# Decode attention beside an MLP on one core: the last K tile and a V tile trade places, and the MLP's first product is spread over three steps

## The chip, the core and the metric

The kernel runs on one core of a Trainium2 chip. It is one launch, and the metric is the device time of that launch in microseconds, lower being better. A core has five engines that run side by side, each with its own queue in program order: TensorE (PE in the profile; its weight loads are PEld), VectorE (DVE), ScalarE (ACT), GpSimd (POOL) and SyncE (SP). Sixteen DMA engines move data between the main memory (HBM) and the core's SBUF; an engine only issues a transfer. Matmuls write to PSUM.

## What is computed

A decode step with one new token for each of 4 sequences. The normalized input goes to two branches whose results are added to it.

```python
x = A_x                                   # [4, 1, 576], bf16
xn = _layernorm(x)
return x + _A_ref(xn, K, V, wq, wo) + _B_ref(xn, w1, w2, w3, w4)

# branch A: 32 query heads, 16 K/V heads, Dh = 128, the last W = 2048 of 8192 rows of the cache
q = (x @ wq) -> [4, 32, 1, 128]
scores = einsum(q, k) * Dh ** -0.5
o = einsum(softmax(scores), v)
A = o.reshape(4, 1, 4096) @ wo

# branch B: with one token per sequence the shifted parts of the mixer are all zeros, so x1 = x
B = x1 + gelu(_layernorm(x1) @ w3) @ w4   # 576 -> 4608 -> 576
```

## The kernel before

**Tiles.** The 16 K/V heads are taken in 8 pairs (`NPR`), called t = 0 to 7. For a pair the 2048 rows of both heads and of all 4 sequences make one K tile and one V tile of 128 partitions x 16,384 bf16, 4 MB each. They share one pool `kv` of three buffers (`NKV = 3`), given out in turn; a load waits until the tile that held its buffer before has been read out.

**Loads.** All of this kernel's large loads but wq are issued from POOL's queue, in order. `order` (L166 to L171) is the sequence of tiles: K0 K1 V0 K2 V1 K3 V2 K4 V3 K5 V4 K6 V5 K7 V6 V7, and at the end W, which stands for the last quarter of wo and the six pieces of w4. `flush_loads` (L174) issues from it as long as a counter of free buffers allows; `free_one` (L189) adds one to the counter and calls it. It is called at two points of a step: after the fourth transpose of a K tile, and after the last P*V of a V tile. So the place of a load in POOL's queue is fixed when the program is built; when it starts is decided by its wait on the reader of its buffer. `load_kv` (L123) gathers 128 rows of 32 KB by an indirect DMA. w4 takes the buffer in which w3 lay.

**A step of the loop** (L582) works on three pairs at once: K of pair t, the softmax and P*V of pair a = t - 1, and the finish of pair o = t - 2.

- `k_transpose(t, q)` (L292), q = 0 to 3: DVE turns a quarter of the K tile in 32 x 32 blocks into one of two `kt` buffers. The first quarter of the next pair is done at the end of a step.
- `k_mask` and `k_scores` (L396, L402): PE writes -1e30 where a row belongs to another sequence, then adds eight matmuls of 128 x 512 for each quarter. A pair has two score tiles in PSUM.
- `sm_max`, `sm_maxT`, `sm_neg`, `sm_back`, `sm_bias`: DVE and PE find the maximum of each head and bring it back to all partitions. `sm_exp` (L443): ACT. `sm_turn` (L452): DVE transposes the exponentials into the `pt` buffers, of which even and odd pairs have one set each. `sm_den`, `sm_rec`: the denominators.
- `pv(t, u, lo, hi)` (L471): 32 matmuls for a pair, issued as four groups of eight between the groups of scores. The result `O` is one of two PSUM buffers.
- `o_scale`, `o_turn`, `o_sum`, `o_expand`, `o_spread`, `o_pick`, `o_proj` (L480 to L530): DVE scales and adds the four parts of `O` (four instructions), PE transposes, DVE sums, and for every second pair the result is spread to four heads' rows and multiplied by a quarter of wo into the accumulator `acc`.

**The MLP's first product**: `mlp_g(r)` (L536), r = 0 to 2, are 20, 20 and 10 matmuls with w3; `mlp_turn(r)` (L551) transposes the results; `mlp_act` (L566) is the gelu, five POOL instructions and one on ACT. All of it is written into step t = 3 (`G_AT`).

**After the loop** (L651 on) come the scores of pair 7, and around them the finish of pair 5, P*V of pair 6, the softmax and P*V of pair 7, the finish of both, and the second MLP product: the matmuls of w4, into `acc` and then into two other accumulators (`sum_matmuls`), in the order in which the pieces of w4 land.

Of the kernel before, what the change touches and what calls it, by code (L numbers as in the profile page):

```python
# [22 lines left out]
def kernel(  # L23
# [143 lines left out]
    for t in range(NPR):  # L167
        order.append(("V", t))
        if t + 2 < NPR:
            order.append(("K", t + 2))  # L170
    order.append(("W", 0))  # L171
    pos = {"n": 0, "free": NKV}

    def flush_loads(upto=P):  # L174
        while pos["n"] < len(order) and pos["free"] > 0 and pos["n"] < upto:
            kind, t = order[pos["n"]]
            if kind == "W":
                load_wo(Hkv // WOQ - 1)
                load_w4()
            else:  # L180
                if kind == "V" and t % 2 == 0 and t + 2 < NPR:
                    load_wo(t // 2)
                load_kv(kind, t)
            if (kind, t) == ("V", 1):
                load_w3()
            pos["n"] += 1
            pos["free"] -= 1
# [104 lines left out]
    def k_transpose(t, q):  # L292
        src = kv_tiles["K", t][:].bitcast(I32)[:, q * QC:(q + 1) * QC, :].rearrange("p c (ib i) -> p ib c i", i=QD)
        kt = ktp.tile([P, 2, QC, QD], I32, tag="kt")
        nc.vector.transpose(out=kt[:], in_=src)  # L295
        kts[t, q] = kt
# [174 lines left out]
    def pv(t, u, lo, hi):  # L471
        if u == 0 and lo == 0:
            O_ps[t] = ps_o.tile([P, NSL, Dh], F32, tag="O", name="O")
        vn = kv_tiles["V", t][:].rearrange("p (u s c) d -> p u s c d", u=NU, s=NSL)
        for c in range(lo, hi):
            rows = slice(c % 2 * 2 * QD, (c % 2 + 1) * 2 * QD)
            nc.tensor.matmul(out=O_ps[t][rows], lhsT=pts[t % 2 * NU + u][:, c, :], rhs=vn[:, u, :, c, :],  # L477
                             start=(u == 0 and c < 2), stop=False, skip_group_check=True)

    def o_scale(t):  # L480
        o = O_ps.pop(t)
        rds = st.pop(("rd", t))
        O_sb[t] = small.tile([P, Dh], F32, tag="O_sb", name="O_sb")
        nc.vector.tensor_scalar(out=O_sb[t][:], in0=o[:, 0, :], scalar1=rds[:, 0:1], scalar2=None, op0=ALU.mult)
        for s in range(1, NSL):
            nc.vector.scalar_tensor_tensor(out=O_sb[t][:], in0=o[:, s, :], scalar=rds[:, s:s + 1], in1=O_sb[t][:],  # L486
                                           op0=ALU.mult, op1=ALU.add)

    def o_turn(t):
        oT = ps_m.tile([P, P], F32, tag="m", name="oT")  # L490
        nc.tensor.transpose(out=oT[:], in_=O_sb.pop(t)[:], identity=ident_f)
        st["oT", t] = oT

    def o_sum(t):
        oT = st.pop(("oT", t))
        k = 2 * t % WOQ
        if k == 0:
            st["on"] = small.tile([P, WOH, B], BF16, tag="on", name="on")
        with nc.allow_low_precision("summed in float32"):
            nc.vector.reduce_sum(out=st["on"][:, k * rep:(k + 2) * rep, :].rearrange("p (e r) b -> p e (r b)", e=2),  # L500
                                 in_=oT[:].rearrange("p (g e s j) -> p e j g s", g=2, e=2, s=NSL), axis=AX.XY)

    def o_expand(h):
        if h % WOQ < WOQ - 1:
            return
        on = st.pop("on")
        x = small.tile([P, B, WOH, WOD], BF16, tag="ox", name="ox")
        nc.vector.tensor_tensor(out=x[:], in0=on[:].rearrange("p h b -> p b h").unsqueeze(3).to_broadcast([P, B, WOH, WOD]),  # L508
                                in1=own[:].unsqueeze(1).unsqueeze(1).to_broadcast([P, B, WOH, WOD]), op=ALU.mult)
        st["ox"] = x  # L510
# [16 lines left out]
    def o_proj(h):  # L527
        if h % WOQ < WOQ - 1:
            return
        acc_matmuls([(op[:, i, :], wo_tiles[h // WOQ][:, i, :]) for i in range(WOR)])  # L530
# [5 lines left out]
    def mlp_g(r):  # L536
        w3 = w_tiles["w3"]
        chunks = G_CHUNKS[r * NQD:(r + 1) * NQD]
        n = chunks[0][2]
        g_ps = (ps_o if r < 2 else ps_m).tile([P, P, n], F32, tag="O" if r < 2 else "m", name="g_ps")  # L540
        for j in range(KJ + 1):
            for g, (e, i0, _) in enumerate(chunks):
                base, k = (j * F + e * (F // 2), j) if j < KJ else (KJ * F, KJ + e)
                cols = w3[:, base:base + F // 2].rearrange("p (q i) -> p q i", q=P)
                nc.tensor.matmul(out=g_ps[g * QD:(g + 1) * QD], lhsT=ln2T[:, k, :], rhs=cols[:, :, i0:i0 + n],  # L545
                                 start=(j == 0), stop=False, skip_group_check=True)
        m = len(chunks) * QD
        g_sb[r] = bigp.tile([P, P, n], F32, tag="g", name="g_sb", bufs=1)
        nc.scalar.activation(out=g_sb[r][0:m], in_=g_ps[0:m], func=ACT.Copy)

    def mlp_turn(r):  # L551
        chunks = G_CHUNKS[r * NQD:(r + 1) * NQD]
        n, m = chunks[0][2], len(chunks)
        gT_all = ps_m.tile([P, n * m, QD], F32, tag="m", name="gT_ps")
        gT_ps = gT_all[:].rearrange("p (u g) x -> p u g x", u=n)
        gs = g_sb.pop(r)
        for u in range(n):
            nc.tensor.transpose(out=gT_ps[:, u].rearrange("p g x -> p (g x)"), in_=gs[0:m * QD, :, u],  # L558
                                identity=ident_f[0:m * QD, 0:m * QD])
        if r < 2:  # L560
            dst = xs[:, r * NFH:r * NFH + 16, :].rearrange("p (g u) b -> p u g b", u=n)
        else:
            dst = xs[:].rearrange("p (g c) b -> p c g b", c=NFH)[:, 16:18]
        nc.vector.tensor_copy(out=dst, in_=gT_ps[:, :, :, 0:B])
# [15 lines left out]
    G_AT = 3  # L580
    k_transpose(0, 0)
    for t in range(NPR - 1):  # L582
        a, o = t - 1, t - 2
        if a >= 0:
            sm_max(a, 1)
        if o >= 0:
            o_scale(o)
        k_transpose(t, 1)
        if t == G_AT:
            mlp_g(0)  # L590
        k_mask(t, 0)
        k_scores(t, 0, 0)
        if a >= 0:
            sm_maxT(a)
            sm_neg(a)
        k_scores(t, 0, 1)
        if a >= 0:
            sm_back(a)
            sm_bias(a)
            sm_exp(a, 0)  # L600
            sm_exp(a, 1)
        k_transpose(t, 2)
        if t == G_AT:
            mlp_g(1)
            mlp_turn(0)
        k_scores(t, 1, 0)
        if o >= 0:
            o_turn(o)
        k_scores(t, 1, 1)
        if a >= 0:  # L610
            sm_turn(a, 0)
        if o >= 0:
            o_sum(o)
            o_expand(2 * o + 1)
        k_transpose(t, 3)
        free_one()
        if a >= 0:
            sm_turn(a, 1)
        if t == G_AT:
            mlp_g(2)  # L620
            mlp_turn(1)
        k_mask(t, 1)
        k_scores(t, 2, 0)
        if a >= 0:
            sm_den(a)
            sm_rec(a)
            pv(a, 0, 0, SC // 2)
        k_scores(t, 2, 1)
        sm_max(t, 0)
        if o >= 0:  # L630
            o_spread(2 * o + 1)
        if a >= 0:
            pv(a, 0, SC // 2, SC)
        if o >= 0:
            o_pick(2 * o + 1)
        if t == G_AT:
            mlp_turn(2)
            mlp_act()
        if t + 1 < NPR:
            k_transpose(t + 1, 0)  # L640
        k_scores(t, 3, 0)
        if a >= 0:
            pv(a, 1, 0, SC // 2)
        k_scores(t, 3, 1)
        if a >= 0:
            pv(a, 1, SC // 2, SC)
            free_one()
        if o >= 0:
            o_proj(2 * o + 1)
# [1 line left out]
    hl = NPR - 1  # L651
    a, o = hl - 1, hl - 2
    sm_max(a, 1)
    o_scale(o)
    k_transpose(hl, 1)
    k_mask(hl, 0)
    k_scores(hl, 0, 0)
# [6 lines left out]
    sm_exp(a, 1)  # L664
    k_transpose(hl, 2)
    k_scores(hl, 1, 0)
    o_turn(o)
    k_scores(hl, 1, 1)
    k_transpose(hl, 3)
    free_one()  # L670
    o_sum(o)
    o_expand(2 * o + 1)
    sm_turn(a, 0)
    k_mask(hl, 1)
    k_scores(hl, 2, 0)
# [2 lines left out]
    sm_turn(a, 1)  # L678
    k_scores(hl, 3, 0)
    k_scores(hl, 3, 1)  # L680
    sm_den(a)
    pv(a, 0, 0, SC)
    sm_max(hl, 1)
    sm_rec(a)
    pv(a, 1, 0, SC // 2)
    sm_maxT(hl)
    sm_neg(hl)
    pv(a, 1, SC // 2, SC)
    sm_back(hl)
    sm_bias(hl)  # L690
    sm_exp(hl, 0)
    sm_exp(hl, 1)
    o_spread(2 * o + 1)
    sm_turn(hl, 0)
    sm_turn(hl, 1)
    o_pick(2 * o + 1)
    sm_den(hl)
    sm_rec(hl)
    o_scale(a)
    pv(hl, 0, 0, SC)  # L700
    pv(hl, 1, 0, SC)
    o_turn(a)
    o_sum(a)
    o_proj(2 * o + 1)
    o_scale(hl)
    o_turn(hl)
    o_sum(hl)
# [49 lines left out]
```

## Time and profile before

| | |
|---|---|
| median of 3 runs | 211.89 us (211.18 to 214.87) |
| the profiled execution's own time | 211.93 us |
| its span, first to last instruction | 210.1 us |
| PE busy | 143.9 us (68%), 854 matmuls |
| DVE busy | 136.9 us (65%) |
| ACT, POOL busy | 23.1 us, 31.3 us |
| moved by DMA | 87.31 MB, mean 415 GB/s over the span |
| mean granted clock of TensorE | 0.86 |

The profile is one execution. Busy time says how long an engine had instructions running, summed over stages that have different limits, so a share of 68% does not say that PE bounds nothing. A timeline line gives the start, the duration, the engine, the line of the code, the operation with its output and inputs, the number of instructions merged into it, and in brackets how long the engine was idle before and what ended that. In the page's rows of 40 slices a digit is the busy share of a slice in tenths. In the chain that ended last a line gives start, duration and what the chain was in at that time.

### The profile page before, as it was taken

The page shows a single profiled execution, that of the slowest core. Times are in us where ns is not written, and L with a number is a line of the kernel's source. Part 1 is how long each engine was busy: PE and PEld are TensorE (multiplying, and loading weights), DVE is VectorE, ACT ScalarE, POOL GpSimd, SP SyncE. Part 2 cuts the span into 40 slices and gives each one's busy share as a digit, 9 for nine tenths or more (in the row PEclk, how much of TensorE's full clock was granted, in tenths as well). Part 3 has the DMA queues.
Part 4 walks back from the last instruction along what each step waited for, and adds up shares of the span by engine and source line. Part 5 has one row for each costly group of instructions (what it writes and reads, how often), then busy time and mean ns, then how long its engine had stood idle before and what let it go on. Part 6 is the DMA issues. An engine that isn't in the chain of part 4 may idle for free.

```text
span 210.1 us, 2145 instructions
## 1 busy us (share of the span) xinstructions
PE 143.9 (68%) x854; PEld 55.7 (27%) x854; DVE 136.9 (65%) x215; ACT 23.1 (11%) x56; POOL 31.3 (15%) x62
## 2 busy tenths in 40 slices
PE   0248197739867950078999796498657947985874
PEld 0013032222213310013443242133213312332342
DVE  5510679993199900297939993998099949795820
ACT  6102500200002001003000200020002000202001
POOL 4680001012200110000124011001100152100000
PEclk9999579985969999555999699969979985699978
DMA  7999999999999999999999999999999999999990
GB/s 300 399 487 412 399 487 415 418 399 480 418 401 436 445 426 443 437 436 405 474 415 405 469 424 417 434 455 412 430 455 418 427 449 413 412 443 418 413 376 14
DMA packets 4154, 87.31 MB, mean 415 GB/s; under 512 B 488, under 2 KB 496, under 8 KB 1200
## 3 DMA queue, kind: packets, MB, share of 16 engines
q0 software_dynamic: 3840, 82.45, 91.3%
q1 hardware_dynamic: 296, 4.72, 5.4%
q8 instruction: 6, 0.10, 0.2%
q14 instruction: 4, 0.03, 0.0%
q10 hardware_dynamic: 8, 0.00, 0.0%
HBM read 87.17 MB, written 0.00 MB: 415 GB/s over the span
## 4 chain that ended last, share of the span: by engine, by line
DMA 49%; PE 22%; DVE 14%; issue 8%; POOL 5%; ACT 0%; POOLq 0%; DVEq 0%; ACTq 0%
DMA kn<-in_A_k_cache_dram,row 25%; DMA vn<-in_A_v_cache_dram,row 24%; PE O L477 8%; PE S L411 7%; DVE kt L295 5%; DVE pt L456 2%; PE g_ps L545 2%; PE acc L228 2%; DVE O_sb L486 2%; POOL kn L125 1%; PE gT_ps L558 1%; PE sum L250 1%; DVE mx L417 1%; DVE ox L508 1%; POOL first L342 1%
## 5 line engine op out<-in xcount | busy, mean ns | idle before, releaser
L411 PE MATMUL S<-kt,qz 128*128 128x512 bf16 x256 | 80.4, 449 | 30.8 <-DVE kt L295 30.5
L295 DVE STREAM_TRANSPOSE kt<-kn 128x2048 int32<-128x2048 int32 x32 | 73.6, 2304 | 40.2 <-DMA kn<-in_A_k_cache_dram,row 37.7
L411 PEld LDWEIGHTS <-qz 128*128 128x128 bf16 x256 | 24.1, 106 | 76.9 <-issue 59.9
L477 PE MATMUL O<-vn,pt 128*64 128x512 bf16 x256 | 34.7, 400 | 4.7 <-DMA vn<-in_A_v_cache_dram,row 3.5
L447 ACT ACTIVATE E<-S,bias 128x512 bf16<-128x512 f32 x16 | 10.8, 683 | 123.6 <-DVE bias L440 123.6
L456 DVE STREAM_TRANSPOSE pt<-E 64x512 bf16<-64x512 bf16 x32 | 22.1, 690 | 1.5 <-ACT E L447 1.2
L125 POOL DMA_INDIRECT vn<-in_A_v_cache_dram,row x8 | 7.7, 958 | 94.5 <-DVE kt L295 90.7
L477 PEld LDWEIGHTS <-pt 128*64 128x64 bf16 x256 | 12.8, 112 | 20.9 <-issue 9.8
L125 POOL DMA_INDIRECT kn<-in_A_k_cache_dram,row x8 | 7.9, 988 | 40.5 <-PE O L477 22.1
L417 DVE TENSOR_REDUCE mx<-S 128x1 f32<-128x512 f32 x16 | 10.7, 672 | 0.1
L486 DVE SCALAR_TENSOR_TENSOR O_sb<-O,rds,O_sb 128x128 f32<-128x128 f32 x24 | 8.4, 351 | 0.8
L435 PE MATMUL bp<-nm,j_row 16*128 16x1 bf16 x8 | 1.3, 160 | 8.6 <-DVE nm L430 8.6
L545 PE MATMUL g_ps<-w_sb,ln2T 128*32 128x512 bf16 (+1 forms) x50 | 5.4, 512 | 2.3 <-DMA w_sb<-in_B_w_dram 2.3
L399 PE MATMUL S<-negbig,ohT 4*128 4x512 bf16 x16 | 6.4, 398 | 0.0
L355 PE MATMUL q_ps<-wq_sb,xnT 128*32 128x512 bf16 x40 | 4.0, 572 | 0.9 <-DMA wq_sb<-in_A_wq_dram 0.9
L723 DVE CAST fin<-sum 4x288 bf16<-4x288 f32 x1 | 0.4, 446 | 6.0 <-PE sum L250 6.0
L163 POOL DMA_DIRECT2D w_sb<-in_B_w_dram x6 | 3.2, 586 | 6.9 <-DMA vn<-in_A_v_cache_dram,row 6.9
L420 DVE TENSOR_SCALAR dm<-sel_g,mx 128x8 bf16<-128x8 bf16 x16 | 3.9, 242 | 0.6
L373 DVE COPY first<-qT_ps 128x64 bf16<-128x64 bf16 x2 | 0.3, 186 | 6.0 <-PE qT_ps L370 6.0
L280 PE MATMUL tp<-ident_bf,first 4*128 4x4 bf16 x8 | 0.6, 173 | 5.0 <-DVE first L267 5.0
L228 PE MATMUL acc<-first,ident_f 4*4 4x288 f32 x4 | 1.1, 656 | 4.1 <-POOL first L342 4.1
L460 PEld LDWEIGHTS dn<-rs,same_j 128*128 128x128 f32 x16 | 2.9, 188 | 3.2 <-ACT E L447 2.0
(105 smaller groups left out, 88.9 us busy)
## 6 DMA issues: line engine op xcount, KB each, us to landing
wo_sb<-in_A_wo_dram POOLq DMA_DIRECT2D x4, 1152.0 KB, 22.8
w_sb<-in_B_w_dram POOLq DMA_DIRECT2D x1, 4608.0 KB, 29.6
wq_sb<-in_A_wq_dram SPq DMA_DIRECT2D x1, 4096.0 KB, 13.7
w_sb<-in_B_w_dram POOLq DMA_DIRECT2D x1, 2592.0 KB, 27.9
w_sb<-in_B_w_dram POOLq DMA_DIRECT2D x2, 576.0 KB, 31.1
w_sb<-in_B_w_dram POOLq DMA_DIRECT2D x1, 1008.0 KB, 29.8
w_sb<-in_B_w_dram POOLq DMA_DIRECT2D x1, 720.0 KB, 31.1
wq_sb<-in_A_wq_dram SPq DMA_DIRECT2D x1, 512.0 KB, 3.2
```

What stands on the lines that cost most here:

```text
L125: nc.gpsimd.indirect_dma_start(tl[:].rearrange("p c d -> p (c d)"), None, k_rows if kind == "K" else v_rows, bass.IndirectOffsetOnAxis(ap= ...
L228: nc.tensor.matmul(out=acc_of(k % 2 * NI + i), lhsT=lhsT, rhs=rhs[:, i * CW:(i + 1) * CW], start=False, stop=False, skip_group_check=True)
L295: nc.vector.transpose(out=kt[:], in_=src)
L355: nc.tensor.matmul(out=q_ps[r][g * QD:(g + 1) * QD, :], lhsT=xnT[:, k, :], rhs=wq_sb[:, col:col + NW], start=(j == 0), stop=False, skip_gr ...
L399: nc.tensor.matmul(out=S_ps[t, u][:].rearrange("p (c k) -> p c k", k=QD), lhsT=ohT[:], rhs=negbig[:].unsqueeze(1).to_broadcast([B, SC, QD] ...
L411: nc.tensor.matmul(out=S_ps[t, u][:], lhsT=qz[:, z0:z0 + P], rhs=kt[:, ib, sl * SC:(sl + 1) * SC, e:2 * QD:2].rearrange("p c k -> p (c k)" ...
L417: nc.vector.reduce_max(out=mx[:], in_=S_ps[t, u][:], axis=AX.X)
L447: nc.scalar.activation(out=E[t, u][:].rearrange("p c k -> p (c k)"), in_=S_ps.pop((t, u))[:], func=ACT.Exp, scale=scale, bias=st["bias", t ...
L456: nc.vector.transpose(out=pts[t % 2 * NU + u][rows, :, e * QD:(e + 1) * QD], in_=e_in[rows])
L477: nc.tensor.matmul(out=O_ps[t][rows], lhsT=pts[t % 2 * NU + u][:, c, :], rhs=vn[:, u, :, c, :], start=(u == 0 and c < 2), stop=False, skip ...
L486: nc.vector.scalar_tensor_tensor(out=O_sb[t][:], in0=o[:, s, :], scalar=rds[:, s:s + 1], in1=O_sb[t][:], op0=ALU.mult, op1=ALU.add)
L545: nc.tensor.matmul(out=g_ps[g * QD:(g + 1) * QD], lhsT=ln2T[:, k, :], rhs=cols[:, :, i0:i0 + n], start=(j == 0), stop=False, skip_group_ch ...
```

## The change

It has three parts. In `order` K of pair 7 moves ahead of V of pair 5: ... V4 K6 K7 V5 V6 V7 W; W no longer counts as needing a free K/V buffer. P*V of pair 5 is left out of step 6 and written after the scores of pair 7, and what follows from it (the finish of pair 5) moves behind it; P*V of pair 6 and of pair 7 come after that, the last one split around the finish of pair 6. The MLP's first product goes from step 3 alone to steps 3, 4 and 5.

As the buffers are given out in turn, K7 now takes the buffer of K5, V5 that of V4, V6 that of K6 as before, and V7 that of K7.

```diff
         if t + 2 < NPR:
             order.append(("K", t + 2))
+    last_k = order.index(("K", NPR - 1))
+    order.insert(last_k - 1, order.pop(last_k))
     order.append(("W", 0))
...
-        while pos["n"] < len(order) and pos["free"] > 0 and pos["n"] < upto:
+        while pos["n"] < len(order) and pos["n"] < upto:
             kind, t = order[pos["n"]]
+            if kind != "W" and pos["free"] == 0:
+                break
...
         k_transpose(t, 2)
+        if t == G_AT + 1:
+            mlp_g(1)
         if t == G_AT:
-            mlp_g(1)
             mlp_turn(0)
...
-        if t == G_AT:
+        if t == G_AT + 2:
             mlp_g(2)
+        if t == G_AT + 1:
             mlp_turn(1)
...
             sm_rec(a)
-            pv(a, 0, 0, SC // 2)
+            if a < NPR - 3:
+                pv(a, 0, 0, SC // 2)
...
-        if a >= 0:
+        if 0 <= a < NPR - 3:
             pv(a, 0, SC // 2, SC)
...
-        if t == G_AT:
+        if t == G_AT + 2:
             mlp_turn(2)
             mlp_act()
...
-        if a >= 0:
+        if 0 <= a < NPR - 3:
             pv(a, 1, 0, SC // 2)
         k_scores(t, 3, 1)
-        if a >= 0:
+        if 0 <= a < NPR - 3:
             pv(a, 1, SC // 2, SC)
             free_one()
...
     sm_max(a, 1)
-    o_scale(o)
     k_transpose(hl, 1)
...
     k_scores(hl, 1, 0)
-    o_turn(o)
     k_scores(hl, 1, 1)
     k_transpose(hl, 3)
     free_one()
-    o_sum(o)
-    o_expand(2 * o + 1)
     sm_turn(a, 0)
...
     k_scores(hl, 3, 1)
+    sm_max(hl, 1)
     sm_den(a)
-    pv(a, 0, 0, SC)
-    sm_max(hl, 1)
+    pv(o, 0, 0, SC // 2)
+    sm_maxT(hl)
     sm_rec(a)
-    pv(a, 1, 0, SC // 2)
-    sm_maxT(hl)
     sm_neg(hl)
-    pv(a, 1, SC // 2, SC)
+    pv(o, 0, SC // 2, SC)
     sm_back(hl)
     sm_bias(hl)
     sm_exp(hl, 0)
     sm_exp(hl, 1)
-    o_spread(2 * o + 1)
+    pv(o, 1, 0, SC)
+    o_scale(o)
     sm_turn(hl, 0)
     sm_turn(hl, 1)
-    o_pick(2 * o + 1)
+    o_turn(o)
+    o_sum(o)
+    o_expand(2 * o + 1)
     sm_den(hl)
     sm_rec(hl)
+    pv(a, 0, 0, SC)
+    o_spread(2 * o + 1)
+    o_pick(2 * o + 1)
+    pv(a, 1, 0, SC)
+    o_proj(2 * o + 1)
     o_scale(a)
-    pv(hl, 0, 0, SC)
-    pv(hl, 1, 0, SC)
+    pv(hl, 0, 0, SC // 2)
     o_turn(a)
     o_sum(a)
-    o_proj(2 * o + 1)
+    pv(hl, 0, SC // 2, SC)
+    pv(hl, 1, 0, SC)
     o_scale(hl)
```

`hl` is pair 7, `a` pair 6 and `o` pair 5 in the part after the loop.

## The prediction

> **What bounds the kernel now.** I read the page first, for the share of the DMA engines and their rate.
>
> ```profile
> DMA  7999999999999999999999999999999999999990
> GB/s 300 399 487 412 399 487 415 418 399 480 418 401 436 445 426 443 437 436 405 474 415 405 469 424 417 434 455 412 430 455 418 427 449 413 412 443 418 413 376 14
> HBM read 87.17 MB, written 0.00 MB: 415 GB/s over the span
> ```
>
> The second row holds no empty slice between the first and the last: the stream of K, V and weights never stops, so work that only waits for it is free. 87.17 MB by 205 us is 425 GB/s. Two things can therefore move the end: a hole in that stream, or work left when it ends. So next I read the timeline of the last 45 us and the end of the chain.
>
> ```profile
> 152.09 2.31 DVE L295 STREAM_TRANSPOSE kt<-kn 128x2048 int32<-128x2048 int32 x1 [5.46 <-DMA kn<-in_A_k_cache_dram,row]
> 163.20 2.31 DVE L295 STREAM_TRANSPOSE kt<-kn 128x2048 int32<-128x2048 int32 x1
> 165.78 0.94 POOL L125 DMA_INDIRECT vn<-in_A_v_cache_dram,row  x1 [15.08 <-DVE kt L295]
> 170.21 0.94 POOL L125 DMA_INDIRECT vn<-in_A_v_cache_dram,row  x1 [3.49 <-PE O L477]
> 171.41 2.31 DVE L295 STREAM_TRANSPOSE kt<-kn 128x2048 int32<-128x2048 int32 x1 [3.08 <-DMA kn<-in_A_k_cache_dram,row]
> 181.35 0.55 POOL L163 DMA_DIRECT2D w_sb<-in_B_w_dram  x1 [6.94 <-DMA vn<-in_A_v_cache_dram,row]
> 182.23 2.31 DVE L295 STREAM_TRANSPOSE kt<-kn 128x2048 int32<-128x2048 int32 x1 [1.36 <-PE S L411]
> 194.29 3.65 PE L477 MATMUL O<-vn,pt 128*64 128x512 bf16 x32 [0.41 <-DVE pt L456]
> ```
>
> K of pair 6 lands at 152.0, K of pair 7 at 171.4. V6 is issued at 165.78, V7 at 170.21. By issue plus time to landing (17.6, 15.3 and 20.5 us in the DMA issues) V5, V6 and V7 land at 161.7, 181.1 and 190.7. Pair 7's P*V starts at 194.3, behind its softmax and not behind V7.
>
> ```profile
> 194.29 3.65 PE O L477 x32
> 201.45 0.26 PE R L518 x4
> 201.70 3.31 PE acc L228 x66
> 205.01 1.16 PE sum L250 x10
> 206.16 0.48 PE sum L255 x4
> 206.65 0.78 PE sum L250 x12
> 207.43 0.44 DVE fin L723
> ```
>
> That is the chain's end: an unbroken run of engine work. The last piece of w4, issued at 181.35, lands 24.6 us later, at 205.95, and the last matmuls do not wait for it. So in the last stage the queue and the engines end about 1 us apart, engines last. From the end of PE (207.43) to the span's end (210.1) are 2.67 us, and the run itself took 211.93: time = PE's end + 4.50. That run stands 0.04 us from the median 211.89.
>
> **Part 1, the MLP in three steps: nothing.** It moves 50 matmuls (L545: 5.4 us in all, 40 of 512 and 10 of 256), 10 transposes and five POOL instructions (108.41 to 111.13), and adds none. In step 3 nothing is gained, as DVE waits for K4 until 110.2 in any case. In step 4 the second chunk (20 matmuls, 2.32 us at half clock) goes ahead of scores that DVE's fourth transpose waits for: V4 is issued at about 126 instead of 123.93, and is needed when the wo piece ahead of it ends at 132.5 (113.36 + 19.1). DVE has 3.30 us idle before K5. In step 5 the third chunk (1.31 us) and its two transposes (0.45) push the end of P*V of pair 4, and with it V5's issue, from 149.77 to 151.5 at the latest; the POOL work of the MLP stands between K7 and V5 in that queue and is over by about 150.5. The stream does not need V5 before K7 has ended near 161. If that 10 us cover were gone, the cost would be these 1.8 us.
>
> **Part 2, K7 before V5.** K7 takes the buffer of K5 and is issued where V5 was, at 144.08, so it lands near 161.7 and V5 near 171.4. V6 keeps its place (165.78): step 6 is a DVE chain without idle time from 152.09 to 168.33, and without P*V of pair 5 (32 matmuls, 4 x 1.05 us) only PE gets lighter. DVE then no longer waits 3.08 us: the first transpose of K7 starts at 168.35 instead of 171.41.
>
> The price: V7 now takes K7's own buffer, so its issue waits for the last transpose of K7. Let T be the end of that transpose. From 168.35: to the second transpose 3.05 (4.48 between 171.41 and 175.89, less 1.43 for the four O_sb operations that leave this place), to the third 2.67 (175.89 to 178.56), to the fourth 2.31 if PE keeps up, 3.67 if it runs at half clock as now (178.56 to 182.23, with the 1.36 wait), and 2.31 for itself. T = 178.7 or 180.05. PE idles from about 167.8 to 170.7 ahead of these scores. The trace has halved clocks after idles of 2.61 (56.8 to 59.4), 2.93 (to 46.87) and 2.0 us (115.1 to 117.1), and none after 2.32 (74.8 to 77.2). I take the middle leaning to half, T = 179.5.
>
> The Trainium skill, in "TensorE: Matmul & The Clock Gate", section "HAM oscillation — how this bites in real kernels", says that PE gaps above about 3.4 us are what throttles; by that rule 2.9 us would be safe, T 178.7 and the engine chain below 0.8 us shorter, but the 2.0 and 2.6 us rows speak against it.
>
> V7's issue is T + 0.27 (165.51 to 165.78 for V6) = 179.8. From issue to first packet no row shows directly. From below: K0 is issued at 8.54, and the packets begun at 11.8 are still the other queue's; one packet is 1.2 us, so 2.1 us at least if the choice falls one packet ahead. From above: V6, issued at 165.78, follows K7's last packets at about 169.2 without a gap, so 3.4 at most. I take 2.7: first packet at 182.5. V6's completion packets come in two bursts, ten engines at 178.8 to 179.6, six at 180.0 to 180.7; the late ones set the end. Hole: 182.5 - 180.5 = 2.0 us (0.3 to 3.2 over both ends of T and of the delay). Behind V7 in POOL's queue stand the wo piece (0.58) and six pieces of w4 (2.70 + 0.55); they go out by 184.6, and the stream needs them after V7, near 191, so they cost nothing. The last w4 piece no longer waits for V6 (6.94 now), as V6 has landed. All of them land 2.0 later: 205.95 + 2.0 = 207.95, then the last few matmuls, about 0.45: **208.4 by the queue**.
>
> "DMA: Bandwidth & Descriptors", Specifications, of the Trainium skill puts the first byte of a GpSimd-issued transfer at about 1 us; by that V7 would start at 180.8, the hole would be 0.3 and the queue would end at 206.7. No run here shows such a start on an empty queue.
>
> **Part 3, the tail.** Three P*V now stand behind the last scores. From T: turn 1.42, maximum and dm 0.96, turn 1.42, maximum and dm 0.96 = T + 4.76; to the bp matmul 1.15 (190.08 to 191.23, eight P*V matmuls in it) = 5.9; the other 16 of P*V 5, 1.92 = 7.85; O_sb 1.5 = 9.35; turns of pair 7 2.84 = 12.2 (they wait for P*V 5, which reads the same pt buffers, and stand behind O_sb on DVE); on and ox 1.0 = 13.2; R 0.26 = 13.45, with the first half of P*V 6 hidden in that stretch; second half 1.9 = 15.35; o_proj 0.6 = 16.0; P*V 7 3.65 and one oT 0.3 = 20.0 (V7, at 192.7, has landed by T + 16.0 = 195.5); from there to the end of R 3.15 (198.54 to 201.70) = T + 23.1 = 202.6, against 201.70 now. So the three P*V behind each other eat what the earlier K7 gave. R to the end of PE was 5.73 (201.70 to 207.43): **208.3 by the engines**. Both ends agree; the later counts: 208.4 + 4.50 = **212.9 us**, +1.0.
>
> **Rivals.**
> *The end gets free (faster).* T = 178.7 and a delay of 2.1 give a hole of 0.6; R ends at 201.8, and PE, not idle before, runs the last products at full clock, where it was at 0.50 from 202.6 to 205.75 (1.6 us). Then the queue decides: 205.95 + 0.6 + 0.2 = 206.75, **211.3**. For it: more PE work right before the end. Against: PE still idles around the last O_sb and ox, as it did at 198.8 to 201.4 before the clock fell. The floor, no hole at all, is 210.7; 2% (4.2 us) cannot be gained, as the bytes must still pass.
> *PE at half clock through the last pair (slower).* Place: the scores of pair 7. With P*V 5 gone from step 6, PE idles more often, and 16 matmuls of slices 2 and 3 take 3.7 per eight instead of 2.0. It decides once the last scores end later than T + 3.8, when DVE wants their maximum; at half clock they end at T + 5.6. T = 180.05, +1.8, +23.1, +5.73 = 210.7, **215.2**. The queue, with the long delay (hole 3.2), would give 209.6. For it: clock 0.50 from 172 to 182 now. Against: PE is denser there than now, without the 3.5 us wait before.
> *The order does not take effect.* If K7 still came last (its issue held behind something on POOL), T would be today's 184.5, V7's first packet 187.5, the hole 7.0: 205.95 + 7.0 + 0.45 + 4.5 = **217.9**. Against: K7's buffer is K5's, read out at 143.8, and nothing slow stands ahead of it.
>
> **How the numbers follow.** Forecast 0.50, free end 0.23, half clock 0.19, no effect 0.05, something else 0.03. The range goes from a nearly free end, 210.8, to past the half-clock case, 215.6; the forecast's own is 211.9 to 214.2. A measurement of this kernel tells about 2% (4.2 us) from no change: above 216.1 lie the no-effect case and a little of the half-clock one, 0.09; below 207.7 almost nothing, 0.02; 0.89 between.
>
> **What would show it.** Right: K7's first transpose at 168 to 169 with no DMA wait, V7's issue at 179 to 180.5 released by a kt transpose, a dip of the DMA share near 181 that was not there, last PE work near 208.4, R's end near 202.6. Part 1 is wrong if a dip of the stream lies before 160. The mechanism is wrong if the stream runs through 181 without a dip, or if the fourth transpose of K7 ends outside 178 to 181.

## The result and the profile after

The changed kernel takes 213.42 us (median of 6 runs, 212.54 to 214.07). The kernel before, run beside it, takes 211.16 (6 runs, 210.70 to 214.87). The ratio is 1.0105 with a 95% interval of 1.0072 to 1.0138: slower by about 1%, less than the 2% that count as a difference here. All ratios leave out the few runs that fell in a slower state (here the 214.87 of the kernel before), which the medians include. The profiled execution of the changed kernel took 212.99 us with a span of 211.2 us, against 211.93 and 210.1 before.

First the page. These are the rows that showed an unbroken stream before.

```profile
DMA  7999999999999999999999999999999998899990
GB/s 299 410 484 397 428 465 419 397 465 428 403 486 438 408 441 410 419 432 465 397 438 453 397 478 436 403 425 459 403 428 465 397 451 379 298 479 387 415 421 29
```

A slice is 5.28 us. The two eights are slices 33 and 34, from 174.2 to 184.8 us. The second of them moved 298 GB/s, where before the same slice had 412. There is no other dip. The timeline tells what lies in that place.

```profile
151.87 2.31 DVE L299 STREAM_TRANSPOSE kt<-kn 128x2048 int32<-128x2048 int32 x1 [5.22 <-DMA kn<-in_A_k_cache_dram,row]
165.56 0.94 POOL L125 DMA_INDIRECT vn<-in_A_v_cache_dram,row  x1 [13.92 <-DVE kt L299]
168.02 2.30 DVE L299 STREAM_TRANSPOSE kt<-kn 128x2048 int32<-128x2048 int32 x1
170.37 1.72 PE L415 MATMUL S<-kt,qz 128*128 128x512 bf16 x4 [2.75 <-DVE kt L299]
174.24 4.49 DVE L299 STREAM_TRANSPOSE kt<-kn 128x2048 int32<-128x2048 int32 x2
179.00 0.94 POOL L125 DMA_INDIRECT vn<-in_A_v_cache_dram,row  x1 [12.50 <-DVE kt L299]
180.53 3.21 POOL L163 DMA_DIRECT2D w_sb<-in_B_w_dram  x6
```

K7's first transpose at 168.02 has no bracket: nothing was waited for, where before there were 3.08 us of waiting for the transfer. The last two transposes are one block that ends at 178.74. V7's issue follows 0.26 later, at 179.00, released by a `kt` transpose; before, it went out at 170.21. The windows show what this did to the transfers. A window counts a packet whole, where it begins, so its DMA share can pass 1. Its columns are: window; its length; busy time and instructions of PE, PEld, DVE, ACT, POOL; the granted clock; the DMA share; GB/s. The kernel before:

```profile
178.00:180.00 2.00, 1.71 (x5) 0.65 (x5) 1.75 (x4) 1.26 (x4) 0.00 (x0) 0.50 0.99 426
180.00:182.00 2.00, 2.00 (x6) 0.59 (x4) 0.87 (x1) 0.19 (x2) 0.55 (x1) 0.50 1.21 524
```

The changed kernel:

```profile
178.00:180.00 2.00, 1.77 (x9) 0.71 (x8) 1.99 (x3) 0.00 (x0) 0.99 (x2) 1.00 0.38 164
180.00:182.00 2.00, 1.85 (x14) 0.94 (x13) 1.94 (x5) 0.00 (x0) 2.00 (x4) 1.00 0.87 262
```

In the packets that begin in these 4 us the kernel before moved 2 x (426 + 524) = 1900 KB, the changed one 2 x (164 + 262) = 852 KB. At the 425 GB/s of the whole stream the missing 1048 KB are 2.5 us, a rough figure, as packets are cut at the windows' edges. How much of it reaches the end is told by the landings. The issues have the time from issue to landing as their last number. The kernel before, issued at 170.21 (V7), 171.15 (the wo piece) and 171.71 (the first piece of w4):

```profile
w_sb<-in_B_w_dram POOLq DMA_DIRECT2D x1, 2592.0 KB, 27.9
wo_sb<-in_A_wo_dram POOLq DMA_DIRECT2D x1, 1152.0 KB, 22.3
vn<-in_A_v_cache_dram,row POOLq DMA_INDIRECT x1, 20.5
```

The changed kernel, issued at 179.00, 179.95 and 180.53:

```profile
w_sb<-in_B_w_dram POOLq DMA_DIRECT2D x1, 2592.0 KB, 21.3
wo_sb<-in_A_wo_dram POOLq DMA_DIRECT2D x1, 1152.0 KB, 14.8
vn<-in_A_v_cache_dram,row POOLq DMA_INDIRECT x1, 13.0
```

V7 lands 1.3 us later than before (192.0 against 190.7) and so does the wo piece (194.75 against 193.46). But all six pieces of w4 land 2.2 to 2.3 us later: 201.86, 204.27, 206.03, 207.43, 207.78 and 208.14, against 199.59, 202.01, 203.83, 205.22, 205.59 and 205.95. So another 0.9 us is added behind the wo piece. The DMA queues of the changed kernel between 197.5 and 198.5 show a second kind of transfer there:

```profile
q8 instruction: 1, 0.02, 6.0%
```

It is one packet of 16 KB (0.02 MB), from 197.71 to 198.67. The stream's last 4-byte packet for a transfer on each engine marks that engine's end of it: for the first piece of w4 fifteen engines end by 200.5 and one at 201.4, and this one is still a microsecond behind at the end (207.8 against 206.7). The kernel before has such an instruction packet too, at 201.33, and no landing moved. There ten engines ran about a microsecond ahead of the other six (V7: 188.6 to 189.1 and 190.0 to 190.3), and by the times of its packets the delayed engine was one of the ten. After the hole all sixteen start V7 nearly together and end it at 190.9 to 191.6, so that lead is gone. The hole therefore costs 1.3 us directly and 0.9 because an engine that is held up has no lead left. The records do not name the engine, so that it is the same packet which delays it is inferred from the times; the run short_pv5 below fits.

Now the end of the chain (start, duration, and what it was in).

```profile
168.02 2.31 DVE kt L299
170.37 1.72 PE S L415 x4
172.20 1.82 PE S L415 x4
174.24 4.50 DVE kt L299 x2
179.00 0.94 POOL vn L125
179.95 0.60 POOL wo_sb L147
180.54 1.55 POOL w_sb L163 x3
182.10 25.33 DMA w_sb<-in_B_w_dram
207.47 1.05 PE sum L254 x12
208.52 0.43 DVE fin L733
```

Before, the chain was engine work from 171.4 on. Now 25.33 us of it are the DMA queue, up to the landing of the fourth piece of w4, and the chain reaches that queue through V7's issue and K7's last transposes. After the end of R (first line), PE's last products wait for pieces of w4:

```profile
201.77 0.27 PE L522 MATMUL R<-sel_i,ox 128*128 128x8 bf16 x4 [1.11 <-DVE ox L512]
206.07 0.78 PE L254 MATMUL sum<-w_sb,gT 128*4 128x288 bf16 x10 [0.53 <-DMA w_sb<-in_B_w_dram]
207.47 1.00 PE L254 MATMUL sum<-w_sb,gT 128*4 128x288 bf16 x12
```

PE ends at 208.52 instead of 207.43. That is +1.09, and the profiled times differ by 212.99 - 211.93 = 1.06.

Why only 1.1 of the stream's 2.2? Before, the last piece had landed at 205.95, which with 0.4 of matmuls would have allowed an end at 206.35 (an estimate). PE ended at 207.43, because its own chain was later. These 1.1 us of slack took up half of the delay.

### The profile page after: what moved, and what is told of

Its sections match the earlier page's. It is cut to its first block, busy times and chain, and to the rows that moved or that the text cites. A ratio compares the mean times of both kernels' runs of the same rounds, so it can differ in the third digit from the quotient of the medians.

```text
span 211.2 us, 2134 instructions
## 1 busy us (share of the span) xinstructions
PE 144.9 (69%) x843; PEld 56.5 (27%) x854; DVE 136.6 (65%) x215; ACT 23.0 (11%) x56; POOL 31.3 (15%) x62
## 4 chain that ended last, share of the span: by engine, by line
DMA 55%; DVE 16%; PE 13%; issue 11%; POOL 3%; ACT 0%; POOLq 0%; DVEq 0%
DMA kn<-in_A_k_cache_dram,row 43%; DMA w_sb<-in_B_w_dram 12%; DVE kt L299 11%; PE S L415 10%; PE O L481 2%; DVE O_sb L490 1%; POOL vn L125 1%; DVE mx L421 1%; POOL w_sb L163 1%; DVE pt L460 1%; PE sum L254 0%; POOL wo_sb L147 0%; POOL rstd L270 0%; DVE row L116 0%; PE S L403 0%
## 5 line engine op out<-in xcount | busy, mean ns | idle before, releaser
L415 PE MATMUL S<-kt,qz 128*128 128x512 bf16 x245 | 82.1, 468 | 33.7 <-DVE kt L299 32.2
L415 PEld LDWEIGHTS <-qz 128*128 128x128 bf16 x256 | 25.1, 110 | 76.5 <-issue 61.1
L481 PE MATMUL O<-vn,pt 128*64 128x512 bf16 x256 | 33.5, 391 | 2.5 <-DMA vn<-in_A_v_cache_dram,row 2.5
L488 DVE TENSOR_SCALAR O_sb<-O,rds 128x128 f32<-128x128 f32 x8 | 2.8, 346 | 5.8 <-PE O L481 5.8
L495 PE MATMUL oT<-ident_f,O_sb 128*128 128x128 f32 x8 | 2.9, 361 | 3.6 <-DVE O_sb L490 3.3
L549 PE MATMUL g_ps<-w_sb,ln2T 128*32 128x512 bf16 (+1 forms) x50 | 4.8, 445 | 0.7 <-DMA w_sb<-in_B_w_dram 0.7
L359 PE MATMUL q_ps<-wq_sb,xnT 128*32 128x512 bf16 x40 | 4.5, 630 | 0.9 <-DMA wq_sb<-in_A_wq_dram 0.9
```

What stands on the lines that cost most here:

```text
L359: nc.tensor.matmul(out=q_ps[r][g * QD:(g + 1) * QD, :], lhsT=xnT[:, k, :], rhs=wq_sb[:, col:col + NW], start=(j == 0), stop=False, skip_gr ...
L415: nc.tensor.matmul(out=S_ps[t, u][:], lhsT=qz[:, z0:z0 + P], rhs=kt[:, ib, sl * SC:(sl + 1) * SC, e:2 * QD:2].rearrange("p c k -> p (c k)" ...
```

## The experiments

The theory is that of the queue: the time is set by the stream, whose hole depends on V7's issue. Each microsecond of later issue costs one, and a V7 that need not wait for K7's last transpose costs nothing. The first rival is that of the engines: the chain of the tail, with three P*V behind each other, sets the end. The second is that of the MLP: its spread delays loads. The kernel before was run again with each batch; its medians were 211.87 for the first four kernels, 211.45 for the next four and 211.82 for the last two.

**mlp_only.** The kernel before with the MLP's three edits alone:

```diff
+        if t == G_AT + 1:
+            mlp_g(1)
         if t == G_AT:
-            mlp_g(1)
...
-        if t == G_AT:
+        if t == G_AT + 2:
             mlp_g(2)
+        if t == G_AT + 1:
             mlp_turn(1)
...
-        if t == G_AT:
+        if t == G_AT + 2:
             mlp_turn(2)
             mlp_act()
```

> The kernel before with only the MLP's first product spread over steps 3, 4 and 5. The theory (the whole loss is a hole in the stream of loads, because V7 is issued only when K7 has been read out, at 179.0 instead of 170.2) expects the time of the kernel before, ratio 0.998 to 1.002, with V4 issued about 2 us later than before and no dip of the DMA share. The rival that the spread MLP costs the time (V4 and V5 issued later, PE busier in steps 4 and 5) expects a ratio near 1.010. If the spread were a gain that the hole hides, it would be below 0.997.

Measured: 211.07 us, ratio 0.9959 (0.9927 to 0.9991). It is not slower, so the rival of the MLP falls; it is even a little below the 0.998 to 1.002 that was expected. V7 is issued at 169.97, and the page of this run has no dip. The profile gives no reason for a gain: its end is the same unbroken engine chain, with the last group of `acc` starting at 203.24 and PE's end at 207.36 (207.43 before).

**order_only.** The changed kernel with the MLP back in step 3.

```diff
-        if t == G_AT + 1:
-            mlp_g(1)
         if t == G_AT:
+            mlp_g(1)
             mlp_turn(0)
...
```

> The changed kernel with the MLP's first product back in step 3 alone: the new order of the loads and the three P*V behind the last scores remain. The theory expects the changed kernel's time, ratio 1.010 (1.007 to 1.014), V7 issued near 179.0, the last w4 piece landing near 207.4. The rival that the MLP costs the time expects 1.000.

Measured: 213.07 us, ratio 1.0066 (1.0034 to 1.0099). The loss is there without the MLP's spread. V7's issue is at 178.65 and PE's end at 208.06, each a little earlier than in the changed kernel (0.35 and 0.46).

```profile
181.72 25.22 DMA w_sb<-in_B_w_dram
206.99 1.07 PE sum L254 x12
208.06 0.44 DVE fin L731
```

**late_kt.** K7's last transpose goes behind one turn of pair 6, so that V7's issue comes later while the work stays the same.

```diff
-    k_transpose(hl, 3)
-    free_one()
     sm_turn(a, 0)
+    k_transpose(hl, 3)
+    free_one()
```

> The changed kernel with the last transpose of K7 one place later, behind the first turn of pair 6 (1.38 us); DVE does the same work in the same total. If the hole sets the end, V7 is issued at 180.4, the last w4 piece lands at 208.8 and the time is 1.4 us above the changed kernel: ratio 1.017 (1.013 to 1.021). If the engines' chain behind the last scores sets it (three P*V after each other), DVE reaches the last maximum at the same time and nothing is lost: 1.010.

Measured: 214.55 us, ratio 1.0115 (1.0075 to 1.0155). The ratio lies below the 1.013 to 1.021 that was expected, partly because the runs of the kernel before had a median of 211.87 in this batch and not 211.16, and partly because the issue came 1.14 us later than in the changed kernel and not 1.4. In microseconds the step holds: issue 178.65 to 180.14 (+1.49) from order_only, and +1.48 in the medians of the same batch. Against the changed kernel itself, which has the same MLP, PE's end moves by the same 1.14 as the issue.

```profile
180.14 0.94 POOL L125 DMA_INDIRECT vn<-in_A_v_cache_dram,row  x1 [13.46 <-DVE kt L299]
```

**gate_v7.** The kernel before, with the old order and the old tail, but V7 held until K7's third transpose by a small copy on POOL.

```diff
                 load_w4()
+            elif (kind, t) == ("V", NPR - 1) and upto == P:
+                break
...
     k_transpose(hl, 2)
+    late = const.tile([1, 1], I32, name="late")
+    nc.gpsimd.tensor_copy(out=late[:], in_=kts[hl, 2][0:1, 0, 0, 0:1])
+    flush_loads(P + 1)
```

> The kernel before, with its old order and its old tail, and one thing added: POOL copies one element of K7's third transposed quarter before it issues V7, so V7 goes out near 181.2 instead of 170.2 although its buffer is free. In the changed kernel an issue at 179.0 made the last w4 piece land 1.5 us later, so here it should land 3.7 later, at 209.6, and PE should end at 210.1 instead of 207.4: +2.7 us, ratio 1.013 (1.009 to 1.017). If the order or the tail of the changed kernel makes its loss and not the late issue, the ratio is 1.000 to 1.002 here.

Measured: 216.18 us, ratio 1.0197 (1.0154 to 1.0240); in the profile 216.03, 4.1 us above before, where 2.7 (1.009 to 1.017) had been expected. A late issue of V7 alone makes the slowdown, in a kernel that has neither the new order nor the new tail. Of the 1.4 us that the size was off, 0.66 are the issue itself, at 181.86 instead of 181.2:

```profile
181.14 0.18 POOL late L669
181.32 0.54 issue
181.86 0.96 POOL vn L125
184.96 25.54 DMA w_sb<-in_B_w_dram
210.54 1.03 PE sum L252 x12
211.56 0.43 DVE fin L728
```

The other 0.7 was an error of the expectation, which had put the changed kernel's stream 1.5 us behind that of before, by setting its fourth piece of w4 (207.43) against the other's sixth (205.95); the 207.4 in other expectations is the same slip. Like with like it is 2.2. This run also shows the delay from issue to first data on a wholly empty queue:

```profile
180.00:182.00 2.00, 1.87 (x9) 0.66 (x7) 2.00 (x2) 0.40 (x2) 0.32 (x2) 1.00 0.00 0
182.00:184.00 2.00, 1.77 (x8) 0.67 (x7) 1.97 (x3) 0.00 (x0) 2.00 (x4) 1.00 0.58 164
```

From 180 to 182 no packet begins (the last of V6 ends at 180.8), and the first of V7 begins at 183.52, 1.66 us after the issue. The four kernels together:

| kernel | V7's issue | PE's end | difference |
|---|---|---|---|
| order_only | 178.65 | 208.06 | 29.41 |
| changed | 179.00 | 208.52 | 29.52 |
| late_kt | 180.14 | 209.66 | 29.52 |
| gate_v7 | 181.86 | 211.56 | 29.70 |

Over 3.2 us of issue the end moves by 3.5, nearly one to one, in two different tails. That is the queue's line. An end set by the engines would not follow the issue in this way: in gate_v7 their tail is that of the kernel before.

**split_v7.** The changed kernel with V7 in two halves. The first half goes into that half of K7's tile which the second transpose has read out, and the other half is issued where V7 was.

```diff
+    def load_half(t, h):
+        tl = kv_tiles["K", t]
+        lo = h * (NC // 2)
+        nc.gpsimd.indirect_dma_start(tl[:, lo:lo + NC // 2, :].rearrange("p c d -> p (c d)"), None, v_rows,
+                                     bass.IndirectOffsetOnAxis(ap=row[:, t:t + 1], axis=0),
+                                     element_offset=lo * Dh)
+        kv_tiles["V", t] = tl
...
-                load_kv(kind, t)
+                if (kind, t) == ("V", NPR - 1):
+                    load_half(t, 1)
+                else:
+                    load_kv(kind, t)
...
     k_transpose(hl, 2)
+    load_half(hl, 0)
```

> The changed kernel with V7 loaded in two halves into K7's own buffer: the first half is issued when the first two transposes of K7 are done (near 173.5), the second after the fourth (179.0). If the hole is the loss, there is none left: the first half keeps the stream busy to 184, the last w4 piece lands at 205.9 to 206.2 as before, and what remains is the engines' chain (R's end near 202): PE ends at 206.5 to 207.7, 0.0 to 1.0 us under the kernel before, ratio 0.995 to 1.001. If the order itself, or the three P*V behind the last scores, makes the loss, the ratio stays at 1.007 to 1.011.

Measured: 211.99 us, ratio 1.0019 (0.9983 to 1.0056), a little above the 0.995 to 1.001 expected: the time of before within what can be told apart. The halves go out at 173.64 and 178.91 and land at 185.9 and 190.7; the last piece of w4 lands at 205.9, as before. So the hole is gone, and PE still ends at 207.66:

```profile
201.68 0.26 PE R L533 x4
201.93 3.59 PE acc L243 x66
205.52 0.87 PE sum L265 x10
206.88 0.78 PE sum L265 x12
207.66 0.43 DVE fin L745
```

This is the engine chain, with the end of R (201.94) near where it was in the kernel before (201.70). The rival of the engines therefore has a true part: without the hole the tail sets the end, at about the time of before.

**short_pv5** and **split_short_pv5.** The changed kernel, and split_v7, with P*V of pair 5 cut to two of its 32 matmuls.

```diff
-    pv(o, 0, 0, SC // 2)
+    pv(o, 0, 0, 2)
...
-    pv(o, 0, SC // 2, SC)
...
-    pv(o, 1, 0, SC)
```

> The changed kernel without 30 of the 32 matmuls of pair 5's P*V (only two are left, so that its output is started): that part of the computation is left out. It takes some 2 to 3 us out of the engines' chain behind the last scores (R's end near 199.5 instead of 202.0) and leaves the loads as they are. If the stream sets the end, nothing is gained: ratio 1.006 to 1.011, last w4 piece at 207.4. If the engines' chain sets it, it falls by 2 us, to 0.998.

> Both of the edits before: V7 in halves, and P*V of pair 5 left out but for two matmuls. The stream's end is again that of the kernel before, and the engines are ahead of it: PE ends some 0.5 us after the last w4 piece, at 206.4, 1.0 us under the kernel before, ratio 0.994 to 0.997. If it is equal to the halves alone, the engines' chain cost nothing there.

Measured: 213.91 us, ratio 1.0101 (1.0051 to 1.0150), and 211.11 us, ratio 0.9987 (0.9964 to 1.0009). Less work in the tail gains nothing while the hole is there. Alone, short_pv5 proves little: R ends at 201.24, not near 199.5 as expected, with PE's clock at 0.50 from 185.3 to 192.1; and PE waits for w4 and then runs its last matmuls at 0.50, so that it ends at 209.66, 1.1 us later than the table's line gives for its issue at 179.04:

```profile
206.12 1.36 PE L254 MATMUL sum<-w_sb,gT 128*4 128x288 bf16 x10 [2.11 <-DMA w_sb<-in_B_w_dram]
```

With the split its PE ends at 206.62, 0.4 us after the last landing (206.25); the ratio is above the 0.994 to 0.997 expected.

short_pv5 has its instruction packet at 202.92, after the first two pieces of w4. These land at 200.90 and 203.31, 1.3 us later than before; the third and the fourth land at 206.08 and 207.46, 2.2 later. This is the step of 0.9 us again, at another place.

**tail_only**, **split_tail** and **split_tail_mlp3.** The same work in another order after the last scores: P*V of pair 6 and of pair 7 are each split around the steps that wait for DVE. tail_only has this alone, split_tail has it with V7 in halves, and split_tail_mlp3 has both with the MLP in step 3.

```diff
     pv(o, 1, 0, SC)
+    pv(a, 0, 0, SC)
     o_scale(o)
     sm_turn(hl, 0)
     sm_turn(hl, 1)
     o_turn(o)
+    sm_den(hl)
+    pv(a, 1, 0, SC)
     o_sum(o)
     o_expand(2 * o + 1)
-    sm_den(hl)
     sm_rec(hl)
-    pv(a, 0, 0, SC)
+    pv(hl, 0, 0, SC)
     o_spread(2 * o + 1)
     o_pick(2 * o + 1)
-    pv(a, 1, 0, SC)
-    o_proj(2 * o + 1)
     o_scale(a)
-    pv(hl, 0, 0, SC // 2)
+    pv(hl, 1, 0, SC)
     o_turn(a)
+    o_proj(2 * o + 1)
     o_sum(a)
-    pv(hl, 0, SC // 2, SC)
-    pv(hl, 1, 0, SC)
```

> The changed kernel, its loads as they are, with the tail in the other order alone (P*V of pair 6 before the transpose of pair 5's output, P*V of pair 7 before R of pair 5). If the stream sets the end, the engines are ready some 3 us earlier (R's end near 198.5) and wait for the last w4 piece, which lands at 207.4 again: ratio 1.006 to 1.011, as for the changed kernel. If the engines' chain had a share in the loss, it falls below 1.004.

> The whole computation: V7 in halves, and the tail written in another order (P*V of pair 6 starts before the transpose of pair 5's output is waited for, P*V of pair 7 before R of pair 5), so that PE does not idle behind the O_sb instructions of pair 5. R's end near 198.5 instead of 202.0, PE's end 0.5 us after the last w4 piece, near 206.4: 1.0 us under the kernel before, ratio 0.994 to 0.997. If PE's clock halves over the last products, or R is not earlier, it is that of the halves alone.

> V7 in halves and the tail in the other order, with the MLP's first product back in step 3. Nothing late in the kernel is left to hide what the spread gives or costs. If it is worth nothing, the ratio is that of the halves with the new tail, 0.994 to 1.000, and the last w4 piece lands at the same time within 0.3 us. If the spread helps the stream, it is 0.3 to 0.5% longer than that.

Measured: tail_only 213.22 us, ratio 1.0084 (1.0053 to 1.0115). R ends at 200.01, 2.0 us earlier than in the changed kernel, and the time does not move. The timeline shows where the 2 us went:

```profile
202.10 2.33 PE L232 MATMUL acc<-w_sb,gT 128*4 128x288 bf16 x36 [2.09 <-DMA w_sb<-in_B_w_dram]
```

They are a wait for w4 of 2.09 us. This is the clean form of what short_pv5 was to show: making the tail 2 us shorter gains nothing in the changed kernel, and the rival of the engines falls for it.

split_tail takes 210.86 us, ratio 0.9966 (0.9936 to 0.9995), and split_tail_mlp3 210.99, ratio 0.9978 (0.9957 to 1.0000). In one batch, tail_only to split_tail_mlp3 is -2.23 us: the full price of the hole, now that no slack of the engines absorbs part of it (the two also differ in the MLP's place; split_tail, which does not, lies at 210.86 in another batch). The windows of split_tail over the old hole:

```profile
178.00:180.00 2.00, 1.77 (x9) 0.71 (x8) 1.99 (x3) 0.00 (x0) 0.97 (x2) 1.00 0.86 369
180.00:182.00 2.00, 1.87 (x14) 0.95 (x13) 1.94 (x5) 0.00 (x0) 2.00 (x4) 1.00 1.01 434
```

Its last piece of w4 lands at 206.0 and PE ends at 206.33, so it stands at the floor that the unbroken stream sets, an estimate from the kernel before: 205.95 + 0.4 + 4.5 = 210.85. It is clearly faster than the changed kernel. Against the kernel before it gains about a third of a per cent, less than the 2% that count: the fastest runs of that kernel take 210.7 as well, but many of its runs take 211 to 213. The MLP's place makes no difference that can be told apart between split_tail and split_tail_mlp3 (their intervals overlap), so what gave mlp_only its 0.4% stays open.

## Why the prediction was right, and which of its terms were off

Forecast: 212.9 us, within 2%, a little slower, through a hole in the stream ahead of V7. Measured: 213.42. The mechanism and the place are shown: the dip, the wait on K7's last transpose, and the slope of nearly one against V7's issue. The size of the hole's price was reached by errors that cancel. By its own steps:

- *Part 1 costs nothing.* V4 is issued at 124.25 (said: about 126), V5 at 150.65 (said: 151.5 at the latest), and no dip lies before 160. mlp_only confirms it.
- *K7's transposes.* The first starts at 168.02, as said. T was put at 179.5 and is 178.74, its lower end. The idle time of PE ahead of these scores, 2.75 us, did come with half clock, as the leaning to half clock supposed: it is 0.50 from 170.6 to 174.0. But it was whole again before the scores that the fourth transpose could wait for, so the 1.36 us wait did not come.
- *From issue to first packet.* Put at 2.7, with 2.1 as the least. It is 1.65: 181.86 to 183.52 in gate_v7, 180.14 to 181.78 in late_kt, 179.00 to 180.64 in the changed kernel. This term failed. Its lower bound came from K0's start behind another queue's packets, which does not bound a start on an empty queue.
- *The hole's reference.* The prediction said that V6's six late engines set the end, and counted from 180.5 to V7's first packet at 182.5. That packet came at 180.64, since the issue was 0.8 earlier and the delay 1.05 shorter than said. With these measured values the prediction's own sum would have been 179.0 + 1.65 - 180.5, about 0.15, and with it "the end gets free". What the sum left out is larger. The first V7 packets took 1.4 to 1.9 us where 1.2 is usual, and two engines began V7 only at 181.4; so V7 landed 1.3 us later and not 0.15. The ten engines that were done with V6 at 178.7 to 179.4 stood idle until 180.6 and lost their lead, which by the times of the packets let the instruction packet add 0.9. In all the stream's end is 2.2 us later (said: 2.0). The size was right by luck.
- *The queue's end.* Said: PE at 208.4. Measured: 208.52.
- *The engines' end.* Said: R's end at T + 23.1, 202.6. Measured: T + 23.3 = 202.04. The sum of the tail holds to 0.2 us, but it is no tie with the queue, as the prediction had it: by the engines alone there was slack, which the waits for w4 and tail_only show.
- *The rivals.* The half clock came (0.50 from 170.6 to 174.0, and again from 201.3 to 204.7), but PE still had to wait for w4 after it. The free end is real, but only when the hole is taken away: split_tail, at 210.86, is near the floor of 210.7 that the prediction gave for no hole at all. The order did take effect.
- *The distance to before.* By profiled executions +1.06 us, as predicted (+1.0). By medians +2.26, since before's median is 211.16 with six runs instead of 211.89 with three: four of the six lie between 210.7 and 211.2. The profiled run of before had PE at clock 0.50 from 202.6 to 206.0, and its end was set by that work; that the shorter runs are those without this is a guess, as no trace of one was at hand.

Of the two rules of the Trainium skill that were weighed: "DMA: Bandwidth & Descriptors", Specifications, puts the first byte at about 1 us. Measured here: 1.65 from the start of the issuing instruction, nearer to the page than to the 2.7 taken from the rows; but the hole of 0.3 that followed from it was wrong as well, by the reference point. "TensorE: Matmul & The Clock Gate", section "HAM oscillation — how this bites in real kernels", puts the harmful gap above about 3.4 us. Here 2.75 us of idle time were followed by clock 0.50, so the rows that the prediction set against it were right.

## What to carry to other kernels

When a stream of transfers is the floor, the last read that frees a buffer is a due time. Here every microsecond of V7's issue between 178.65 and 181.86 cost about one. The last piece landed 29.14 us after the issue, against 205.95 in the unbroken stream; if the line goes on below 178.65, which no run tests, an issue up to about 176.8 would have been free. Swapping two loads changes which reader they wait for: follow the buffers, not the order of the list, and look if half of the buffer is free earlier, which here took the whole loss away (173.6 instead of 179.0 for the first half). Slack on the other side absorbs part of a loss once: take it from the distance between the queue's end and the engines' end, and expect the next microsecond to cost in full.

## What the runs showed of the hardware that was not expected

- An indirect gather on an empty queue moves its first packet 1.64 to 1.66 us after its issue (changed kernel, late_kt, gate_v7), of which 0.94 to 0.96 is the issuing instruction. The first packets behind such a pause took 1.4 to 1.9 us each in the changed kernel, the later ones 1.2.
- The sixteen engines do not end a gather together. In the changed kernel V6's completion packets come in two bursts, ten at 178.7 to 179.4 and six at 180.2 to 180.7, and its landing is at 181.16. A transfer that goes out only for the second burst leaves ten engines idle.
- Such a lead of some engines hides delays. An instruction packet of 16 KB takes 0.94 us on one engine; with the lead gone, the pieces of w4 behind it landed 0.9 to 1.0 us later still (changed kernel, late_kt, gate_v7; in short_pv5 from the third piece on). That the packet is the cause is inferred from the times.
- After 2.75 us without matmuls PE's clock was at 0.50 from 170.6 to 174.0, and full again in time for the work that counted.
